# Second MLP product of round 4 moved to three one-pass products, each round's second product a round behind its first, and a new instruction order

## The chip, the cores and the metric

One core of a Trainium2 chip runs the whole kernel. The metric is device time in microseconds, the median of the timed runs. Engines: TensorE (PE: matmuls, and weight loads as PEld), VectorE (DVE), ScalarE (ACT), GpSimd (POOL) and SyncE (SP, which issues nearly all DMAs).

## What is computed

An RWKV-6 attention followed by a layer norm and an MLP with a residual, all in float32, on 4 sequences of 768 steps, 8 heads of 48, model width 384, hidden width 1536:

```
for t in range(S):                                   # per batch and head
    cur = outer(u * k[t], v[t])
    y[t] = r[t] @ (state + cur)
    state = w[t][:, None] * state + outer(k[t], v[t])
x  = y, heads joined to (4, 768, 384)
xn = (x - mean) / sqrt(var + 1e-6) * g_ln
out = x + relu(xn @ w_ch1) @ w_ch2
```

## The kernel before

**Rounds.** The 3072 steps are cut in 8 rounds of 384 steps (`RN`), each three tiles of 128 (`TT`). A round has an attention part (`front`: loads, inner products of four steps, transposes, four levels of `quads` and `grow`, `states`, `outputs`) and an MLP part (`back`: `normalize`, `turn_x`, then `mlp`). The first product has 12 blocks f of 128 hidden units (`FC`), each a PSUM bank `h_ps`; the second sums over the 12 blocks into three output tiles i.

**Two kinds of product.** A full float32 matmul, or three one-pass matmuls on values split beforehand into a high part H, a low part L and a combination D (names `xhl`, `xd`, `wh`, `wl`, `w1diff` for the first product, `hH`, `hL`, `hD`, `w2h`, `w2l`, `w2d` for the second). Rounds 1 to 7 take the first product in one-pass form (`THREE = 1`). Rounds from `LAST = NR - 3` = 5 on take the second in one-pass form too (`thirds`); rounds 0 to 4 use full matmuls `o<-ffn,h`. The third of the split weights `w1diff` goes to DRAM once and is streamed back for every block (`stream`).

**The one-pass second product before.** In `thirds`, ScalarE writes H from the bank `h_ps` (Relu), VectorE writes L from the same bank and then D. The three take the twelve homes "h". Each output tile has two sums: D's in one bank (the minus part) and L's and H's in another. Tiles 0 and 1 take the two-bank homes "a" (which attention uses until its end), tile 2 two homes "b", each a bank of its own. After the last block VectorE adds the two sums to x (`add`, `rest`) and SP stores the tile. In the last round's last block `go_d` and `go` are planned apart for all three tiles.

**What sets the order.** `Plan` collects operations with their needs and buffers; the list `ORDER`, written out in the file, says in which order they are issued, and for some which of two engines takes them (an entry over 10000 names the second engine). Buffers come from `HOMES`. Every engine works its own queue in this order. Where TensorE would pause for more than 0.35 us by the plan, matmuls on zeros named `idle` are put in. All engine instructions are recorded by one helper, so every row of the profile says L47; tiles tell them apart.

## Time and profile before

| | |
|---|---|
| median of 3 runs | 494.89 us (493.52 to 494.91) |
| the profiled execution | 493.06 us, span 491.2 us |
| busy PE / PEld | 480.1 us (98%) / 402.2 us (82%) |
| busy DVE / ACT / POOL | 352.8 us (72%) / 256.3 us (52%) / 105.5 us (21%) |
| TensorE clock granted | 1.00 over the span |
| DMA | 56.21 MB, mean 114 GB/s |
| full second products `o<-ffn,h` | 360 records, 125.2 us busy |

A page row gives engine, operation, output and inputs, count, then busy time and mean duration of one, then the idle time of the engine just before the group and what ended it. A full float32 matmul leaves two records. The `idle` matmuls count as busy.

### The profile page before, as it was taken

The numbers are of one execution on the slowest core, as the hardware profiler recorded it, in microseconds if no ns is written. First come the engines' busy times: TensorE is split into PE (matmuls) and PEld (weight loads), VectorE is DVE, ScalarE is ACT, GpSimd is POOL, SyncE is SP. The second block draws the span as 40 slices with busy tenths as digits, with TensorE's granted clock in tenths as the row PEclk, the third lists the DMA queues.
The fourth block names the chain that finished last, engine by engine and source line by source line (L and its number), as shares of the span: only waits on it lengthen the run. The fifth ranks groups of instructions, "written<-read, shape, count | busy, mean of one in ns | idle before, by whom it ended". The sixth has DMA issues, their size and how long they took to land.

```text
span 491.2 us, 17021 instructions
## 1 busy us (share of the span) xinstructions
PE 480.1 (98%) x7354; PEld 402.2 (82%) x7354; DVE 352.8 (72%) x735; ACT 256.3 (52%) x580; POOL 105.5 (21%) x107
## 2 busy tenths in 40 slices
PE   8998999999999999999999999999999999999995
PEld 4776887668987779966799667998679999999995
DVE  7998999999948999478737598366467766345334
ACT  2989988745573358434255712656454434332330
POOL 6423503612514026107700300000001100000000
PEclk9999999999999999999999999999999999999999
DMA  6777686377660455482177201740321142122201
GB/s 207 212 202 200 164 267 148 112 218 172 154 177 5 99 150 170 108 210 47 33 192 189 62 12 30 166 101 11 65 58 35 48 129 66 48 85 90 84 0 51
DMA packets 105435, 56.21 MB, mean 114 GB/s; under 512 B 61840, under 2 KB 102288, under 8 KB 105360
## 3 DMA queue, kind: packets, MB, share of 16 engines
q1 hardware_dynamic: 105088, 54.92, 42.4%
q8 instruction: 58, 0.95, 0.8%
q10 hardware_dynamic: 272, 0.20, 0.1%
q14 instruction: 17, 0.14, 0.1%
HBM read 45.27 MB, written 7.47 MB: 107 GB/s over the span
## 4 chain that ended last, share of the span: by engine, by line
PE 78%; DVE 7%; ACT 6%; DMA 3%; POOL 2%; issue 2%; SPq 1%; POOLq 0%; DVEq 0%; ACTq 0%
PE h_ps L47 28%; PE a L47 19%; PE o L47 19%; PE o_2P L47 3%; PE r_ps L47 2%; PE k_ps L47 2%; SPq L47 1%; PE xT_ps L47 1%; PE o_2D L47 1%; DMA raw<-in_moe_w_ch_dram 1%; PE kn_ps L47 1%; DVE A L47 1%; ACT k L47 1%; DVE vals L47 1%; ACT held L47 1%
## 5 line engine op out<-in xcount | busy, mean ns | idle before, releaser
L47 PE MATMUL o<-ffn,h 128*128 128x384 f32 x360 | 125.2, 489 | 0.1
L47 PEld LDWEIGHTS o<-ffn,h 128*128 128x128 f32 x360 | 65.0, 190 | 35.5 <-DVE ffn L47 0.4
L47 ACT ACTIVATE h_ps<-h_ps 128x384 f32<-128x384 f32 x84 | 39.4, 475 | 70.8 <-PE h_ps L47 67.8
L47 DVE SCALAR_TENSOR_TENSOR hL<-h_ps,hH 128x384 fp32r<-128x384 f32 x36 | 20.0, 557 | 50.3 <-ACT hH L47 50.2
L47 PE MATMUL h_ps<-xd,d 128*128 128x384 f32 x228 | 54.9, 353 | 0.4 <-DVE xd L47 0.3
L47 PE MATMUL h_ps<-xhl,wl 128*128 128x384 f32 x216 | 51.8, 348 | 0.0
L47 PE MATMUL h_ps<-xhl,wh 128*128 128x384 f32 x216 | 49.6, 337 | 0.0
L47 PEld LDWEIGHTS a<-r,k 48*56 48x56 f32 (+3 forms) x3072 | 39.4, 122 | 9.7 <-issue 5.9
L47 PE MATMUL a<-r,k 48*56 48x32 f32 (+3 forms) x3072 | 43.5, 208 | 0.5 <-DVE k L47 0.4
L47 ACT ACTIVATE h<-h_ps 128x384 f32<-128x384 f32 (+2 forms) x72 | 30.2, 441 | 23.6 <-PE h_ps L47 23.2
L47 PEld LDWEIGHTS h_ps<-xd,d 128*128 128x128 f32 x228 | 39.8, 188 | 2.9 <-issue 0.4
L47 PEld LDWEIGHTS h_ps<-xhl,wl 128*128 128x128 f32 x216 | 37.9, 188 | 1.1
L47 PEld LDWEIGHTS h_ps<-xhl,wh 128*128 128x128 f32 x216 | 38.8, 188 | 0.0
L47 DVE TENSOR_TENSOR r<-r,tot 112x768 f32<-112x768 f32 (+1 forms) x40 | 32.5, 817 | 7.2 <-PE a L47 7.2
L47 ACT ACTIVATE hH<-h_ps 128x384 fp32r<-128x384 f32 x36 | 17.7, 491 | 34.8 <-PE h_ps L47 34.8
L47 DVE TENSOR_TENSOR k<-k,tot 112x768 f32<-112x768 f32 (+1 forms) x40 | 32.4, 815 | 4.1 <-PE a L47 3.2
L47 PE MATMUL h_ps<-xf,w 128*128 128x128 f32 (+1 forms) x144 | 25.9, 333 | 0.1
L47 PE MATMUL a<-w2l,hL 128*128 128x384 f32 x72 | 24.4, 338 | 1.4 <-DVE x L47 1.4
L47 PE MATMUL idle<-nought 128*128 128x384 f32 (+2 forms) x74 | 24.8, 465 | 1.0 <-DVE eps L47 1.0
L47 ACT ACTIVATE xf<-xT_ps,g_sb 128x384 f32<-128x384 f32 (+2 forms) x27 | 14.5, 546 | 20.4 <-PE xT_ps L47 18.5
L47 DVE COPY_PREDICATED A<-mask,a 128x768 f32<-128x768 int8 (+2 forms) x27 | 24.1, 892 | 1.3 <-PE a L47 1.2
L47 ACT COPY k<-k_ps 112x512 f32<-112x512 f32 x24 | 14.1, 587 | 20.7 <-PE k_ps L47 20.6
(154 smaller groups left out, 1070.0 us busy)
## 6 DMA issues: line engine op xcount, KB each, us to landing
d<-w1d SPq DMA_DIRECT2D x84, 192.0 KB, 2.7
raw<-in_moe_w_ch_dram SPq DMA_DIRECT2D x24, 384.0 KB, 3.7
nat_w<-in_w_dram SPq DMA_DIRECT2D x24, 192.0 KB, 3.8
nat_r<-in_r_dram SPq DMA_DIRECT2D x24, 192.0 KB, 3.8
v<-in_v_dram SPq DMA_DIRECT2D x24, 192.0 KB, 3.5
nat_k<-in_k_dram SPq DMA_DIRECT2D x23, 192.0 KB, 3.7
out_dram<-x SPq DMA_DIRECT2D x5, 576.0 KB, 4.4
w1d<-w1diff SPq DMA_DIRECT2D x12, 192.0 KB, 2.8
```

Source lines behind the costliest of these rows:

```text
L47: ins = self.tc.keep_in_program_order(f(*args, **kw))
```

## The change

- `LAST` becomes `NR - 4`: round 4's second product is one-pass too (36 full products become 108 one-pass ones).
- The first product of a one-pass round now evicts h to SBUF (`relu`, homes "h", as in the other rounds). `thirds` makes H from that copy on ScalarE, L as a plain difference on VectorE or POOL, and D on VectorE; the three take the twelve homes "w2", in which the second product's weights stood before they were split.
- `back(rnd)` no longer calls `thirds`; it is planned after the next round's first products could begin, so that a round's second product lies about a round behind its first.
- The split weights of the second product get new places (`w2_place`), in buffers of the attention that are free by then.
- In the last block, only tile 2 has `go_d` apart from `go`.
- `idle`: the count at the start is worked out up to `WARMED` = 5.9 us.
- `ORDER` is a new list, for all engines. From how the instructions stand: on VectorE, round 1's inner products come earlier and the weights' joins later; the first normalised tile is the 86th VectorE instruction of the plan and was the 77th. The very first loads go r, r, w, ... where they went w, r, w, .... Of the 48 instructions that write L, 24 are on POOL.

```diff
-    THREE, LAST = 1, NR - 3
+    THREE, LAST = 1, NR - 4
...
+    def w2_place(n, f):
+        i = "HLD".index(n)
+        if f < 4 or 6 <= f < 10:
+            q = f >= 6
+            return ("k", "r", "A")[i], f"w2{n}{q:d}", 4, f - 6 * q
+        if f < 6:
+            return ("nk", "nr")[f - 4], f"xw2_{f}", 3, i
+        if f == 10:
+            return "v", "w2_10", 3, i
+        return ("tot", "w2_11", 2, i) if i < 2 else ("vx", "w2D_11", 1, 0)
...
         def high():
             ACT.activation(
-                out=tile_("h", H_, [P, RN], F32R), in_=tiles[h_], func=AF.Relu, scale=TOP
-            )
-        def low():
-            DVE.scalar_tensor_tensor(
-                out=tile_("h", L_, [P, RN], F32R), in0=tiles[h_], scalar=0.0,
-                in1=tiles[H_].bitcast(F32), op0=ALU.max, op1=ALU.subtract,
-            )
+                out=tile_("w2", H_, [P, RN], F32R), in_=tiles[h_], func=AF.Copy, scale=TOP
+            )
+        def low(e):
+            BY[e].tensor_tensor(
+                out=tile_("w2", L_, [P, RN], F32R), in0=tiles[h_], in1=tiles[H_].bitcast(F32),
+                op=ALU.subtract,
+            )
...
-        plan.add("ACT", 0.492, high, r=[h_], w=[H_], pri=at(rnd, 30))
-        plan.add("DVE", 0.557, low, r=[h_, H_], w=[L_], pri=at(rnd, 30), port=True)
+        plan.add("ACT", 0.522, high, r=[h_], w=[H_], new=[("w2", H_)], pri=at(rnd, 30))
+        plan.add(EITHER, (0.55, 1.0), low, r=[h_, H_], w=[L_], new=[("w2", L_)], pri=at(rnd, 30))
...
-            if last and rnd == NR - 1:
+            if last and rnd == NR - 1 and i == 2:
...
-            if rnd >= LAST:
-                thirds(rnd, f)
-                continue
             plan.add("ACT", 0.49, relu, r=[ps], w=[h_], pri=at(rnd, 30))
...
-        if rnd < LAST:
+        if rnd <= LAST:
             back(rnd)
     for f in range(FC):
         halve2(f)
     for rnd in range(LAST, NR):
-        back(rnd)
+        if rnd > LAST:
+            back(rnd)
+        for f in range(FC):
+            thirds(rnd, f)
```

## Prediction

> **What bounds the kernel now.** First the busy shares of the page, then three stages: the opening, the middle, and what is left once the last attention output of the last round is issued (TensorE, 368.23 us, two groups, done at 371.2).

> Stages (us, then busy time and instructions of each engine, granted clock, DMA share, GB/s):

> ```profile
> 0.00:48.80 48.80, 43.68 (x802) 31.58 (x802) 42.13 (x115) 36.45 (x88) 21.01 (x44) 1.00 0.75 204
> 48.80:371.20 322.40, 321.48 (x5906) 257.39 (x5899) 247.88 (x497) 179.18 (x406) 78.66 (x58) 1.00 0.47 119
> 371.20:491.20 120.00, 114.97 (x658) 113.23 (x654) 62.82 (x125) 40.71 (x87) 5.85 (x5) 1.00 0.21 65
> ```

> TensorE (first busy column) is full from 48.8 us on; VectorE (third) has 74 us to spare in the middle and 57 in the last stage. Who TensorE waits for:

> ```profile
> PE xT_ps L47 <- DVE xn L47: 2.3, 2, 2.2
> PE a L47 <- DVE x L47: 1.4, 1, 1.4
> PE idle L47 <- DVE eps L47: 1.0, 1, 1.0
> PE k_ps L47 <- POOL pad_k L47: 1.0, 1, 1.0
> ```

> Under 7 us in all. But a busy TensorE is not always one at work: it also runs "idle" matmuls. I therefore added up the useful matmuls in queue order at their rows' durations. Before 48.8 us they make 17.0 us, so 31.8 us are no work. That gap is 34.4 when the second output group of round 1 starts (62.1 us of work ahead of it, start 96.5), 36.7 at round 2's first group (114.5, 151.2), 40.3 at round 4's (209.0, 249.3), 45.3 at round 7's (322.9, 368.2). It grows by some 2 us a round, spread over the switches between small and full matmuls, with no stall. So in this kernel TensorE work taken away after 48.8 us comes off the end in full, if the opening keeps its pace and nothing new stalls.

> The rows that price the change:

> ```profile
> L47 PE MATMUL o<-ffn,h 128*128 128x384 f32 x360 | 125.2, 489 | 0.1
> L47 PE MATMUL a<-w2l,hL 128*128 128x384 f32 x72 | 24.4, 338 | 1.4 <-DVE x L47 1.4
> L47 ACT ACTIVATE h<-h_ps 128x384 f32<-128x384 f32 x48 | 22.7, 488 | 20.7 <-PE h_ps L47 20.4
> L47 POOL TENSOR_TENSOR w1diff<-wl,wh 128x384 fp32r<-128x384 f32 x7 | 8.4, 1206 | 11.0 <-DVE wl L47 11.0
> ```

> **1. The product of round 4.** In the chain three full products (six records) take 1.94 us, a few 2.13; three one-pass products take 0.53:

> ```profile
> 221.50 1.45 PE a L47 x96
> ...
> 225.98 3.89 PE o L47 x12
> ...
> 479.05 0.53 PE a L47 x3
> ```

> A round has 36 full products, 12 × 1.94 = 23.3 us; they become 36 × 0.527 = 19.0 (18.9 from six in 1.05). Gain 4.3; with one group in six at 2.13 it is 4.7. I take 4.4. [...]

> **2. The last tiles.** Before, the last product of tile 0 is split: the minus part first, then the rest, in the two banks of one tile. The chain shows what this did:

> ```profile
> 484.85 0.72 PE a L47 x4
> 485.57 0.34 issue
> 485.90 1.03 DVE x L47 x2
> 486.93 0.04 issue
> 486.98 0.63 PE a L47 x2
> 487.61 0.02 issue
> 487.63 0.56 DVE x L47
> ```

> The last two matmuls wait for VectorE's read of the other bank, and VectorE ends at 488.19. After, only tile 2, in banks of its own, is split; tiles 0 and 1 run whole. The same matmuls then end at 485.57 + 0.36 = 485.93, the two adds follow 0.33 later and take 1.03: 487.29. Gain 0.9. Bounds: 0 if VectorE still has tile 0's adds in hand (two at 0.55 ahead of tile 1's, but tile 0 ends two product groups earlier), 1.4 if all of the wait goes. Taken 0.9.

> **3. What rides along.** Rounds 5 to 7 evict h first (36 × 0.49 on ScalarE), and round 4 gains 12 high parts (0.52): 23.9 us more on ScalarE, whose busy time is 41 of the last 120 us. Round 4's 12 low parts, 12 differences and 3 more adds are 14.9 us on VectorE, with 57 spare there. The high part stands in ScalarE's queue ahead of the next shrink, for which TensorE's next first product waits; the cover is that thirds run behind their first product (the order has several other groups between). The bank of h_ps is read by one instruction instead of two; TensorE waits for no such bank now, so 0. The twelve "w2" homes hold H, L and D of four f, as "h" did. Round 4's one store of 576 KB becomes three of 192 KB; SP has only the streams of w1diff behind them, and DMA is at 0.21 there. All 0 in the sum; each costs what is shown below under the second rival if its cover is gone. In the new order round 7's attention is issued after 302 us of work instead of 323. [...]

> **4. The opening, found anew.** This is the unknown. Before, VectorE sets it: busy 42 of 48.8 us, and its waits are short ones:

> ```profile
> 13.36 1.03 DVE L47 TENSOR_TENSOR nat_k<-nat_k,nat_r 128x768 f32<-128x768 f32 x1 [1.35 <-ACT pad_k L47]
> 38.46 0.56 DVE L47 BATCH_NORM_STATS2 stats<-x 128x6 f32<-128x384 f32 x1 [1.85 <-ACT x L47]
> ```

> I added VectorE's instructions in queue order at row durations, less the 0.08 us by which neighbours overlap. Before, the first normalised tile is its 77th, 30.1 us of work, done at 40.76: a lag of 10.7. After, round 1's inner products stand ahead of it and the weights' joins behind: the first product of round 0 waits for the 94th, 41.1 us of work. The new place of the normalisation should avoid both waits above (3.2 us), and w's first load, now third in SP's queue (issued at about 2.3 instead of 0.8), costs about 0.6 of that again. So the lag is 8 to 10.7 and this product starts at 49.1 to 51.8, with 16.2 us of work ahead of it: a gap of 32.9 to 35.6, against 31.8. Check at round 1's second output group: VectorE's work up to its scan is the same (80.5 for 80.3), TensorE's work ahead of it is 57.3 for 62.1. With the old lag there (80.3 done at 94.85: 14.5) it starts at 96.7, a gap of 39.4 against 34.4: 5.0 lost. [...] Bounds 0.2 and 5.0. I take 1.5, nearer the low end, since both waits lie before the point.

> **Sum.** −4.4 − 0.9 + 1.5 = −3.8: span 487.4, and with the 1.86 us outside the span (493.06 − 491.2) 489.3. That execution stood 1.83 below the median of the timed runs, so the forecast is 494.89 − 3.8 = **491.1 us**, by itself 489.5 to 493.0.

> **Rivals.**
> *The opening eats the gain.* VectorE keeps its old lag, the new order has 4.8 us less TensorE work ready by round 1, and 5.0 go there: −4.4 − 0.9 + 5.0 = −0.3, 494.6. For it: VectorE's sums at that point are equal. [...]
> *POOL is late in the last rounds (slower).* Of the 48 low parts 24 now run on POOL, each between a high part and a difference that TensorE needs. The row above says 1.00 us undisturbed and up to 1.76 beside VectorE (w2d, alike, 1.2 on average). Toward the end a low part has some 0.7 us in hand: H9 of round 7 gets its home when f = 6 is done, and its product is about 3 us of TensorE work later, while high, low and difference take 0.52 + 1.0 + 0.55 and their hand-overs. If half of the 24 come 0.75 late: 9 us, 500.1; it decides from 3.8/24 = 0.16 us a piece on TensorE's path. Against: VectorE is half idle there and other groups stand between. [...]
> [...]

> **How the numbers follow.** 0.3% or 1.5 us is about what a measurement of this kernel tells from no change: faster is below 493.4, slower above 496.4. Chances: forecast 0.50, opening 0.20, POOL 0.15, more 0.15. Faster: 0.46 of the forecast's, all of the last, 0.03 of the opening's: 0.64. Same: the rest of the forecast's, 0.13 of the opening's, 0.02 of POOL's: 0.19. Slower 0.17. The range goes from 488.3 to 497.0, leaving out half of the last case and most of POOL's.

> **What would show it.** Right: TensorE's round-1 output groups near 91 to 94 us; o<-ffn,h falls from 360 records to 288 (72 per round); the last output group of round 7 near 350; no TensorE wait of over 1 us after it, and the two last adds back to back behind the last matmul. Wrong: round 1's groups at 96 or later; TensorE waiting for hL, hD or hH in the last 130 us; a VectorE or ScalarE wait between 250 and 350, where attention is now packed closer.

## The result, and the profile after

Four timed runs of each kernel, side by side: **490.02 us** (489.85 to 490.25) after, 494.2 (493.28 to 494.91) before, ratio 0.9917 (95% interval 0.9895 to 0.9939): 4.2 us less. The forecast was 491.1. The profiled execution, however, went only from 493.06 to 490.19 us, its span from 491.2 to 488.5: 2.75 us less by the unrounded spans (491.24, 488.48). Both are taken up below; they are not the same thing.

The stages of the changed kernel (us, then busy time and instructions of TensorE, its weight loads, VectorE, ScalarE and GpSimd, granted clock, DMA share, GB/s), the opening, the middle and the end. The last cut lies at the start of round 7's attention outputs here; before, it lay at their end (371.2):

```profile
0.00:48.80 48.80, 42.63 (x709) 30.66 (x713) 43.71 (x116) 34.96 (x79) 21.21 (x41) 1.00 0.72 192
48.80:350.00 301.20, 300.93 (x5775) 246.44 (x5766) 251.08 (x507) 178.09 (x410) 62.27 (x53) 1.00 0.52 130
350.00:488.50 138.50, 134.26 (x946) 133.29 (x945) 71.89 (x131) 60.98 (x138) 29.64 (x27) 1.00 0.18 57
```

TensorE is as full in the middle as before. From the start of round 7's outputs (350.13, before 368.38) to the end it is 138.35 us for 122.86, 15.5 more: round 4's second product and others now lie there. What TensorE waits for, longest first:

```profile
PE w_ps L47 <- POOL w L47: 1.2, 1, 1.2
PE w_ps L47 <- DVE w L47: 1.1, 1, 1.1
PE idle L47 <- DVE eps L47: 1.0, 1, 1.0
PE a L47 <- DVE k L47: 0.9, 1, 0.9
```

None is for `hH`, `hL` or `hD`, and the wait for `xn` (2.3) is gone. The product's rows, in the page's form (busy, mean ns of one, idle before):

```profile
L47 PE MATMUL o<-ffn,h 128*128 128x384 f32 x288 | 99.2, 488 | 0.0
L47 POOL TENSOR_TENSOR hL<-h,hH 128x384 fp32r<-128x384 f32 x24 | 26.8, 1127 | 86.8 <-PE o_2D L47 21.1
L47 DVE TENSOR_TENSOR hL<-h,hH 128x384 fp32r<-128x384 f32 x24 | 14.5, 606 | 13.7 <-PE o_2P L47 5.0
```

72 records (36 full products) have left `o<-ffn,h`. The end of the chain:

```profile
482.20 0.57 DVE x L47
482.77 0.02 issue
482.80 1.03 DVE x L47 x2
483.83 0.02 issue
483.85 1.03 DVE x L47 x2
484.88 0.02 issue
484.91 0.56 DVE x L47
```

No matmul waits for an add any more. All three tiles finish so close together that VectorE does the six adds in one row; it ends at 485.47, the last matmul at 484.27.

**Where the 2.75 us are.** I take the first `a<-last,r` matmul of the output groups of rounds 1, 3, 5 and 7, and subtract the useful TensorE work queued ahead of it at its rows' durations:

| | round 1 | round 3 | round 5 | round 7 |
|---|---|---|---|---|
| before: start, work | 91.91, 57.8 | 200.67, 161.7 | 303.44, 260.6 | 368.38, 322.9 |
| after: start, work | 93.68, 55.8 | 199.39, 157.0 | 293.87, 248.0 | 350.13, 302.2 |
| gap before | 34.1 | 39.0 | 42.8 | 45.5 |
| gap after | 37.9 | 42.4 | 45.9 | 47.9 |

The new opening is 3.8 us dearer at round 1 and 2.4 at round 7. The total of useful work falls from 440.4 to 436.1, by 4.3. From round 7's outputs to the end it is 122.86 us before and 138.35 after, 15.49 more for 16.4 more work: 0.9 less at the tail. −4.3 + 2.4 − 0.9 = −2.8.

This is one pair of profiles. A second profile of the changed kernel (fifth experiment) has a span of 489.8 us at the same clock, 1.3 more; between rounds 3 and 5, where two waits of 0.7 and 0.8 us marked "issue" lie, it loses 1.9. So the sum shows where the time lies, and 2.75 itself is good to about a microsecond.

### The profile page after: what moved, and what is told of

Its sections match the earlier page's. It is cut to its first block, busy times and chain, and to the rows that moved or that the text cites. A ratio compares the mean times of both kernels' runs of the same rounds, so it can differ in the third digit from the quotient of the medians.

```text
span 488.5 us, 17306 instructions
## 1 busy us (share of the span) xinstructions
PE 477.8 (98%) x7412; PEld 410.4 (84%) x7412; DVE 366.7 (75%) x753; ACT 274.0 (56%) x624; POOL 113.1 (23%) x120
## 4 chain that ended last, share of the span: by engine, by line
PE 87%; DVE 5%; SPq 1%; issue 1%; DMA 1%; DVEq 0%
PE h_ps L47 33%; PE a L47 23%; PE o L47 18%; PE o_2P L47 3%; PE r_ps L47 2%; PE o_2D L47 2%; PE xT_ps L47 2%; PE k_ps L47 2%; PE kn_ps L47 2%; SPq L47 1%; DVE A L47 1%; DVE s L47 1%; DVE x L47 1%; DVE k L47 1%; DMA d<-w1d 1%
## 5 line engine op out<-in xcount | busy, mean ns | idle before, releaser
L47 PE MATMUL o<-ffn,h 128*128 128x384 f32 x288 | 99.2, 488 | 0.0
L47 ACT ACTIVATE h<-h_ps 128x384 f32<-128x384 f32 (+2 forms) x108 | 47.7, 454 | 54.8 <-PE h_ps L47 54.2
L47 PEld LDWEIGHTS o<-ffn,h 128*128 128x128 f32 x288 | 52.3, 190 | 29.1
L47 ACT ACTIVATE h_ps<-h_ps 128x384 f32<-128x384 f32 x84 | 38.8, 475 | 49.0 <-PE h_ps L47 47.0
L47 DVE SCALAR_TENSOR_TENSOR hD<-hH,hL 128x384 fp32r<-128x384 f32 x48 | 30.4, 651 | 34.8 <-PE a L47 16.9
L47 PE MATMUL h_ps<-xd,d 128*128 128x384 f32 x204 | 50.0, 353 | 0.3 <-DMA d<-w1d 0.3
L47 PEld LDWEIGHTS a<-r,k 48*56 48x56 f32 (+3 forms) x3072 | 39.7, 122 | 10.1 <-issue 3.1
L47 POOL TENSOR_TENSOR hL<-h,hH 128x384 fp32r<-128x384 f32 x24 | 26.8, 1127 | 86.8 <-PE o_2D L47 21.1
L47 PE MATMUL a<-r,k 48*56 48x32 f32 (+3 forms) x3072 | 44.1, 208 | 1.1 <-DVE k L47 0.9
L47 PE MATMUL h_ps<-xhl,wl 128*128 128x384 f32 x180 | 43.8, 351 | 0.0
L47 DVE TENSOR_TENSOR k<-k,tot 112x768 f32<-112x768 f32 (+1 forms) x40 | 37.8, 947 | 5.9 <-PE a L47 4.5
L47 PE MATMUL h_ps<-xhl,wh 128*128 128x384 f32 x180 | 41.4, 338 | 0.0
L47 PEld LDWEIGHTS h_ps<-xd,d 128*128 128x128 f32 x204 | 35.4, 188 | 2.9 <-issue 0.9
L47 DVE TENSOR_TENSOR r<-r,tot 112x768 f32<-112x768 f32 (+1 forms) x40 | 34.1, 854 | 0.6 <-PE a L47 0.2
L47 PEld LDWEIGHTS h_ps<-xhl,wh 128*128 128x128 f32 x180 | 32.3, 188 | 0.0
L47 PEld LDWEIGHTS h_ps<-xhl,wl 128*128 128x128 f32 x180 | 31.0, 188 | 1.1 <-ACT h_ps L47 0.2
L47 PE MATMUL idle<-nought 128*128 128x384 f32 (+1 forms) x96 | 28.7, 425 | 1.0 <-DVE eps L47 1.0
L47 ACT ACTIVATE hH<-h 128x384 fp32r<-128x384 f32 x48 | 24.4, 522 | 8.0 <-PE a L47 3.5
L47 DVE COPY_PREDICATED A<-mask,a 128x768 f32<-128x768 int8 (+2 forms) x27 | 24.1, 893 | 5.6 <-PE a L47 5.5
L47 PE MATMUL h_ps<-xf,w 128*128 128x128 f32 (+1 forms) x144 | 26.0, 331 | 0.0
L47 PEld LDWEIGHTS idle<-nought 128*128 128x128 f32 x96 | 17.3, 200 | 9.1 <-issue 1.5
L47 DVE TENSOR_TENSOR hL<-h,hH 128x384 fp32r<-128x384 f32 x24 | 14.5, 606 | 13.7 <-PE o_2P L47 5.0
```

Source lines behind the costliest of these rows:

```text
L47: ins = self.tc.keep_in_program_order(f(*args, **kw))
```

## Experiments

Times are medians; where nothing else is said, before ran beside them, at 492.8 to 495.1. "The changed kernel" as a control (fifth experiment) gave 489.48.

**1. The old opening with the new rest.** The entries of `ORDER` up to round 1's second output group are the old ones:

```
-    ORDER = [3, 271, 2, 1, 12, 10, ...]            # new order
+    ORDER = [1, 3, 2, 10014, 13, ...,              # 580 entries of the old order
+             ...]                                  # the rest near the new order
```

> The changed kernel's code, but its order follows the old one instruction for instruction up to the last output group of round 1; the rest keeps roughly the new order, smoothed behind the seam. Theory (the opening cost more than the forecast's 1.5: net 2.65, and 4.1 where round 1 ends; TensorE work decides from there on): round 1's second output group is back at a gap of about 34.4 us between its start and the work queued ahead of it (new order: 38.5), and the gap saved stays to the end in good part: span 484.4 to 485.9, 2.6 to 4.1 less than the changed kernel, time about 486 to 487.5. Rival (what the old opening saves is lost again behind it, because TensorE then waits for VectorE, whose weight joins are still to be done): the gap is smaller at round 1 but equal by round 3; span 487.5 or more.

Measured: 495.04 (491.37 to 498.43), ratio 1.0031 (0.9998 to 1.0064); profiled span 490.4. At round 1 the lead is there: start 92.24, gap 34.4. At round 3 the gap is 42.5 (196.82, 154.3), the new order's. So the rival holds in its times: the lead is gone by round 3, 1.4 us of it right behind the seam. But the waits there are for ScalarE's `r` (two of 0.7, ended at 102.7 and 104.1) and not for VectorE, as the rival had it; where the rest goes is not shown. Eleven of the twelve runs had a clock of 0.985 to 0.995; the one at 1.0 took 492.49, so the clock alone does not explain it. That order is neither kernel's, so this run does not price the opening; it shows that the old opening can't be put ahead of the new rest for free.

**2. Round 4's product as one full matmul in place of three one-pass ones.**

```
             def both(i=i):
+                if rnd == LAST:
+                    PE.matmul(out_tiles(i)[0], tiles[H_].bitcast(F32)[:, ts(i, P)],
+                              w2_part("H", f).bitcast(F32), start=first, stop=last)
+                    return
```

> The changed kernel with round 4's three one-pass matmuls replaced in place by one full-precision matmul of the high parts (the low parts' products are left out, so the output is not the reference's); order, evictions and splits unchanged. Theory (TensorE work after 48.8 us goes to the end in full; a full product costs 0.647 against three of 0.176): 36 x (0.647 - 0.527) = 4.3 us slower than the changed kernel, 494.3. [...] Rival 'in the new order round 4 has slack on TensorE': under 2 us slower, below 492.

Measured: 493.84, against 489.43 for the third kernel on the same chip: 4.4 more. The chain of this kernel prices the product:

```profile
356.73 2.58 PE a L47 x8
```

Eight records are four full products: 0.645 each. From round 7's first `a<-last,r` (351.65) to the end it took 142.63 us, where the changed kernel takes 138.35: **4.28 more, and 36 × (0.645 − 0.527) = 4.25.** The theory holds, to the end in full. A full product costs 0.645/0.176 = 3.7 one-pass matmuls here.

**3. All low parts on VectorE.** The 24 entries of `ORDER` for `low` that name GpSimd lose their 10000.

> The changed kernel with all 48 low parts on VectorE: the 24 that ran on GpSimd (mean 1.13 us) are moved, nothing else. Theory (the low parts on GpSimd are off TensorE's path: no wait for hL, hD or hH in the trace): within 1 us of 490.0 either way; VectorE gains 24 x 0.55 = 13 us where it has over 60 idle. The forecast's rival (a low part that is late on GpSimd holds TensorE up): faster by 2 us or more, below 488.

Measured: 489.43, ratio 0.9919 (0.989 to 0.9948), where the changed kernel has 0.9917 and 0.9915. No change: the low parts on GpSimd were off TensorE's path. What they do cost shows in the rows of this kernel:

```profile
L47 DVE TENSOR_TENSOR hL<-h,hH 128x384 fp32r<-128x384 f32 x48 | 27.2, 580 | 24.1 <-PE a L47 10.2 <-ACT hH L47 6.1 <-PE o_2D L47 4.2
L47 DVE SCALAR_TENSOR_TENSOR hD<-hH,hL 128x384 fp32r<-128x384 f32 x48 | 26.7, 570 | 20.0 <-PE a L47 14.5 <-PE o_2P L47 3.6 <-PE o_2D L47 1.2
```

`hD` takes 570 ns a piece here and 651 in the changed kernel, 3.9 us of VectorE time over 48, all of it in cover. The means hide how: in the changed kernel six of the 48 take 1.18 to 1.37 us, here one does, and the others have about 0.55 in both. Each of these seven began while a GpSimd instruction ran and ended 0.41 to 0.42 us behind that instruction's end.

**4. The kernel before with tile 0 whole in the last block.**

```
-            if last and rnd == NR - 1:
+            if last and rnd == NR - 1 and i:
```

The entry of the separate piece falls out of `ORDER`, and the later numbers there move up.

> The kernel before with one edit: in the last round the last product of tile 0 is no longer split, so that VectorE's read of the minus bank stands behind all six matmuls; all else as before. Theory (the last two matmuls waited 1.43 us for a read of the other bank of their tile): the last two adds start together behind the last matmul, 0.9 us less than before (between 0.4 and 1.4), about 493.6 where before is 494.5. Rival (the adds of tile 2, still in VectorE's queue, set the end): no change, within 0.3 us.

Measured: 491.78, before 492.98, ratio 0.9971 (0.9949 to 0.9993). VectorE's last adds in this kernel:

```profile
483.43 0.55 DVE L47 SCALAR_TENSOR_TENSOR x<-o_2D,x 128x384 f32<-128x384 f32 x1
484.43 0.56 DVE L47 SCALAR_TENSOR_TENSOR x<-o_2P,x 128x384 f32<-128x384 f32 x1 [0.46 <-PE a L47]
484.91 1.14 DVE L47 SCALAR_TENSOR_TENSOR x<-a,x 128x384 f32<-128x384 f32 x2
```

The two last adds run together. From round 7's outputs to the end: 122.07, against 122.86 in the profile of before and 122.85 to 122.87 in two more profiles with that tail (sixth and ninth). That is 0.8, near the 0.9: tile 2's last add, still in the queue (the second line), may hold the other 0.1.

**5. The changed kernel again**, no edit.

> The changed kernel once more, as a control on the chip of these four runs, with more runs of both kernels. Expected: 489 to 490.5, ratio 0.992 +- 0.002, granted clock 0.998 to 1.0 in every run; the kernel before spreads over 491.8 to 496 with mean clocks from 0.987 to 1.0, its longer runs being those with the lower clock.

Measured: 489.48 (488.72 to 491.53), ratio 0.9915 (0.9888 to 0.9942); clock 0.998 to 1.0 in all six. Of before's 17 runs, 12 had a clock of 0.987 to 0.996, and all nine above 493.8 are among them. With the runs of before beside the first, eleventh and twelfth kernels there are 71: 37 with a mean clock of 0.997 or more, median **492.5**; 34 below it, median **494.7**. The changed kernel and those with its opening, or one near it (second, third, seventh, eighth), have 41 runs, every one at 0.997 or more.

**6. Before with the pause at 38.5 us filled.** The longest pause in the old opening is 2.16 us in before's profile, ahead of the first transpose of `xn`; nine more units of idle matmuls go there:

```
-    out.append(lambda n=n, home=home: idle[2](n, home[1]))
+    out.append(lambda n=n + 9 * (op.i == 97), home=home: idle[2](n, home[1]))
```

> The kernel before with one edit: nine more units of idle matmuls (about 1.9 us) where TensorE stands still for 2.4 us at 38.5 us, waiting for the first normalised tile. Theory (that pause makes the clock fall for a window of 3.4 us in some runs, and these are the kernel's longer ones): clock 0.997 or more in every run, the runs above 494 vanish, the median falls by 0.5 to 1.2 us against before, its fastest runs stay at 491.8. Rival (the spread comes from the loads, the clock only goes with it): spread and median as before, within 0.3.

Measured: 494.6, before 493.84; ratio 1.002 (0.9996 to 1.0044). The pause is filled (TensorE is busy for 3.40 of the 3.41 us from 38.85 on), yet six of twelve runs have 0.986 to 0.996 and 495.8 to 497.5. The theory falls: this pause alone is not what makes before's long runs long.

**7. w first.**

```
-    ORDER = [3, 271, 2, 1, 12, ...]
+    ORDER = [1, 3, 271, 2, 12, ...]
```

> The changed kernel with w's first load back at the head of SP's queue (order of the first loads as before). Theory (the opening is late because VectorE's first steps wait 1.5 us for w): the wait goes, the first product of round 0 starts 1 to 1.5 us earlier than 51.7, and the end with it: 0.8 to 1.5 us faster than the changed kernel in the same call. Rival (r and k then land later, and VectorE waits for these instead): no change within 0.4, the wait appears at another tile.

The changed kernel's wait that this aims at, from its timeline:

```profile
6.52 0.36 DVE L47 TENSOR_TENSOR pad_k<-nat_k,nat_w 128x192 f32<-128x192 f32 x1 [1.50 <-DMA nat_w<-in_w_dram]
```

Measured: 490.17 (488.36 to 490.89), the control 489.48 (488.72 to 491.53). In the profile the first product starts at 49.67 (50.2 to 51.7 in four profiles with w third) and round 1's outputs at 91.67 (92.2 to 93.7), so the opening does gain about 1.2. The time shows nothing of it: between rounds 3 and 5 alone, profiles of one and the same order differ by 2 us (94.0 to 96.4). Not settled.

**8. Another order for the changed kernel**, found by many small moves under the planner's own costs.

> The changed kernel with another order: the same operations, the listed order moved in many small steps so that by the planner's own costs each round's attention output comes about 1 us earlier from round 0 on. Theory (TensorE's queue alone decides once the opening is over, so an earlier opening passes to the end): round 1's first output group 0.7 us earlier than in the changed kernel (93.5), the end as much: 489.0 to 489.5. Rival (the planner's 1 us is below what its costs are wrong by): within 0.5 either way, with new waits for VectorE.

Measured: 490.1 (489.84 to 490.61): no gain. Round 1's first output group came at 94.97, not 0.7 earlier but 1.3 later than in the changed kernel. The rival holds: a planned microsecond is less than what the plan's costs are wrong by.

**9 and 10. Two more profiles, in search of the clock**: the kernel before, and the kernel of the first experiment, both without an edit.

> The kernel before, unchanged, for another profile: about half of its runs show a mean clock of 0.987 to 0.996 and are 1 to 4 us longer, and the profile on hand is one of the others. Theory (the new opening keeps the clock where the old one lets it fall): a run with the lower clock shows one to four windows of 3.4 us at half clock, all before 60 us, and the time lost there. Rival (the clock falls in the middle of the kernel): the windows lie behind 60 us, where the two kernels hardly differ.

> The first experiment's kernel (old order up to round 1's last output, then the new one), unchanged, for another profile: 11 of its 12 runs had a clock of 0.985 to 0.995. The same theory and rival as for the kernel before: windows at half clock before 60 us, and round 1's outputs later by what they cost (two windows or more, 97 us or later for the first), or windows behind 60 us.

Measured: 493.28 (clock 0.993) and 500.25 (0.986). Each row is a stretch of the trace; the third column from the right is the granted clock. Kernel before:

```profile
37.63:41.04 3.41, 1.05 (x8) 0.75 (x7) 2.54 (x6) 3.33 (x11) 0.67 (x2) 1.00 0.86 152
41.04:44.45 3.41, 3.41 (x75) 3.02 (x74) 2.89 (x10) 3.16 (x9) 0.86 (x1) 0.50 0.98 311
```

A stretch with 1.05 us of work is followed by one at half clock. Round 1 came 0.4 us later than in the first profile of before (92.31 for 91.91), the end 0.2 (span 491.45 for 491.24). The tenth:

```profile
102.60:106.00 3.40, 2.01 (x28) 1.23 (x26) 3.40 (x8) 2.07 (x4) 0.00 (x0) 1.00 0.84 232
106.00:109.40 3.40, 3.12 (x82) 2.75 (x83) 2.16 (x8) 0.53 (x2) 0.00 (x0) 0.50 0.81 161
...
341.50:344.90 3.40, 1.61 (x102) 1.49 (x95) 0.31 (x1) 2.62 (x7) 0.00 (x0) 1.00 0.12 40
344.90:348.30 3.40, 3.40 (x29) 3.31 (x21) 2.70 (x6) 1.16 (x3) 0.00 (x0) 0.50 0.43 86
```

Here the clock is at half from 41.1 to 44.6, from 106.0 to 112.8 and from 344.9 to 348.3. Time goes at the second and the third of these. Round 1 to round 3 takes 107.55 us, in the first experiment's profile, which kept the clock there, 104.58; round 5 to round 7 takes 61.76 for 58.13, with a wait of 1.79 us marked "issue" ahead of the window. The first experiment's profile has the same two waits for ScalarE; in stretches laid 3.41 us apart from its own at half clock (41.47 to 44.88), TensorE is busy for 2.74 and 2.41 us there, and the clock stays full:

```profile
99.49:102.91 3.42, 2.74 (x12) 1.65 (x13) 3.33 (x9) 2.15 (x5) 0.00 (x0) 1.00 0.51 133
102.91:106.32 3.41, 2.41 (x92) 1.88 (x93) 3.41 (x11) 2.01 (x4) 0.00 (x0) 1.00 0.74 195
```

So both readings hold in part: windows at half clock fall before 60 us and cost little, and behind it, at about 1.5 to 1.8 us each if all of these differences, less that wait, are theirs. The stretches at half clock in these two traces and in those of the first, eleventh and twelfth experiments are 3.4, 6.8, 13.7 and 17.1 us long, one, two, four and five times 3.41. Within one trace their starts lie whole numbers of 3.41 us apart, to 0.2 us (41.1, 106.0 and 344.9 in the tenth: 19 and 70 of them; 10.7, 34.6 and 266.7 in the eleventh: 7 and 68).

**11. The changed kernel without fillers between about 29 and 46 us.**

```
-                    out.append(lambda n=n, home=home: ...)
+                    if not 30 < t < 50:
+                        out.append(lambda n=n, home=home: ...)
```

> The changed kernel without the idle matmuls that fill TensorE's pauses between about 29 and 46 us; the rest of the order is untouched. Theory (in the new opening it is a TensorE that is hardly ever still that keeps the clock): the clock falls to half for one to four windows of 3.4 us right behind, mean 0.985 to 0.997, and the time grows by 1 to 5 us, 491 to 495. Rival (the fillers do nothing here): clock 0.998 or more, time within 0.5 us of 489.5, or a little less.

Measured: **506.25** (504.41 to 507.94), 16.8 above the control of the fifth experiment; mean clock 0.976 to 0.979. Far more than the theory's 5. The clock is at half from 10.7 to 14.1, from 34.6 to 48.2 and, right behind the longest of the waits below, from 266.7 to 270.1. But round 1's outputs start at 93.63, no later than in the changed kernel (93.68); the 14 us are lost behind it. TensorE's waits from 60 us on:

```profile
PE a L47 <- issue: 10.2, 9, 2.4
PE h_ps L47 <- ACT hH L47: 1.1, 1, 1.1
```

Nine waits, eight of them 0.65 to 2.4 us long, that no other engine ends, all in or beside stretches of small matmuls. The changed kernel has none above 0.5 there; the control has two, of 0.7 and 0.8.

**12. The same fillers, but narrow.** As many idle matmuls as in the changed kernel, those of that stretch 8 to 24 columns wide:

```
-                    out.append(lambda n=n, home=home: idle[2](n, home[1]))
+                    out.append(lambda n=n, home=home, t=t: idle[2](n, home[1], 8 if 30 < t < 50 else 128))
...
-    def idle(n, home):
+    def idle(n, home, cols=P):
...
-                t[:, 0 : now * P], zeros, nought.broadcast_to([P, now * P]), ...
+                t[:, 0 : now * cols], zeros, nought.broadcast_to([P, now * cols]), ...
```

> The changed kernel with the same idle matmuls as it has, in the same places and number, but those between about 29 and 46 us are 8 to 24 columns wide instead of 128 to 384: TensorE's queue holds the same instructions, and is still in the pauses. It parts two readings of the run without these matmuls, which took 506 us. Theory A (leaving them out moved where in TensorE's queue the pieces of its program end; the 10 us of waits marked 'issue' in the stretches of small matmuls, 95 to 365 us, come from that): those waits are as in the changed kernel, at most 2 us in all, and the time is 488.5 to 491.5, although the clock is at half for one to four windows between 34 and 48 us; round 1's first output group stays near 93. Theory B (a TensorE that is still in the opening costs the time, through its clock): 495 us or more, clock 0.976 to 0.985.

Measured: **491.55** (489.93 to 494.88), clock 0.977 to 0.986. TensorE's waits from 60 us on in this kernel:

```profile
PE h_ps L47 <- DMA d<-w1d: 0.3, 1, 0.3
PE a L47 <- DVE A L47: 0.3, 1, 0.3
PE a L47 <- issue: 0.2, 1, 0.2
```

The 10 us of "issue" are gone with the instructions back in their number, although the clock is at half for five windows, 33.3 to 50.3 us. Theory A holds in the main: it had said four windows at most, round 1's outputs near 93 (they came at 94.65) and 491.5 at most. 14.7 of the 16.8 us went with the instructions that were missing from TensorE's queue, and about 2 are left for the clock. (The two runs were on different chips; by their ratios to before, 1.025 and 0.9965, the first part is 14.)

What the waits are for, the traces tell, though "issue" names nothing. One DMA queue of the kind "instruction" (q8) brings 58 packets of 16 KB in every one of these profiles, one for each 254 to 256 of TensorE's recorded instructions. All 16 waits of TensorE marked "issue" that are 0.3 us or longer and lie behind 60 us, in six profiles (first, fifth, sixth, seventh, tenth, eleventh), end 1.2 to 1.6 us after one of these packets has landed; waits that another engine ended do so anywhere from 0.3 to 10 us after one. By these times TensorE waited for the next piece of its own program. Leaving 72 instructions out (36 matmuls and as many weight loads), at one packet for about 255, shifts where each later piece begins. That is not all that decides: the changed kernel's first profile has no such wait, its second has two.

## Why the prediction was right or wrong

- **What bounds the kernel** (TensorE's queue behind the opening): right. Work put back in the second experiment came through to the end to 0.03 us.
- **1, the product** (−4.4): right. 4.25 to 4.28 by the second experiment. Of the choice between 4.3 and 4.7, the lower end was the true one. The case "more" of the chances did not come: the price of a full product, 0.645, left no more than these 4.25 to come off.
- **2, the last tiles** (−0.9): right. 0.9 by the changed kernel's trace, 0.8 by the fourth experiment. The lower bound's reason, adds still in VectorE's hand, is there; the two figures leave 0.1 for it.
- **3, what rides along** (0): right. No wait for H, L or D in the trace, no change in the third experiment. The rival of GpSimd being late falls. The six `hD` of 1.18 to 1.37 us lie beside the path. "1.00 us undisturbed and up to 1.76 beside VectorE" was misread: all seven `w1diff` on GpSimd in the profile of before ran beside VectorE work, five at 1.00 us, one at 1.68 (84.47) and one at 1.76 (87.47). From 60 us on TensorE waits only once in the changed kernel's profile, for 0.3 us: VectorE and GpSimd do not hold it up there.
- **4, the opening** (+1.5): this term was mis-sized. It is 3.8 at round 1 and 2.4 at round 7; over the three profiles of the old opening unfilled and with its own rest (before, fourth, ninth) and four of the new one (after, second, third, fifth) the mean gaps at round 7 are 45.1 and 48.1, 3.0 apart. I had reckoned that both old waits (3.2 us) go and that w's later load costs 0.6; the waits went, but w cost 1.50 and 0.43, and the first product came at 51.7, the late end of my 49.1 to 51.8. No run shows the lower bound of 0.2, near which I took the term; the traces show 2.4 to 3.8 in its place. "The opening eats the gain" was thus more than half true. Of its signs, the first output group of round 1 came at 93.7, between 91 and 94; the second, at which I had priced the term, came at about 95, between what I had called right and wrong.
- **The sum** was −3.8 and is −2.75.
- **From the profile to the median: the step that failed unseen.** I took the 1.83 us by which before's profiled execution lay under its median as something that the change leaves alone. Most of it is probably clock, though the runs of that median have no clock on record. In later runs before's executions at a mean clock of 0.997 or more have a median of 492.5, the others 494.7; all 10 runs of the changed kernel are at 0.998 or more, median 489.86, and its profiled execution lies 0.17 above its first median. Clock is not all that parts a profiled execution from its median: in the second and fifth experiments it lies 2.2 and 2.0 us above, at a clock of 1.0. Like with like, the change is 492.53 − 489.86 = 2.67 us, the 2.75 of the profile; the rest of the 4.2 goes with the clock, which the new order lost in none of its runs. So one error took 1.05 us too much off, the other left 1.83 on, and 0.3 more lies in the 0.17 and in the time outside the spans (1.82 before, 1.71 after): 491.1 for 490.0 is a sum right in its large terms and lucky in the rest.
- **Still open:** what starts the windows in before's runs at 0.987. No profile of such a run was caught. The pause at 38.5 us alone isn't it (sixth); the first experiment's kernel, which has this opening and another rest, loses them behind round 1 (tenth). And whether the 1.2 us of w's place can be had.

No version here beats the changed kernel by more than the runs scatter.

## What to carry to other kernels

Where one engine's queue sets the time, a product's price can be taken from the rows to a few hundredths of a microsecond per piece, and comes through in full (here 4.28 us for the 4.25 of the rows); the order of the opening can't (here 2.4 to 3.8 for 1.5), so give it the whole range that its rows allow. Before you subtract a sum from a median, ask why the profiled run lies off the median: list every run's granted clock, because a new order may change that as well. And an edit that takes instructions out of TensorE's queue moves all behind it (here 36 idle matmuls fewer went with 16.8 us, and narrow ones in their place took 14.7 of these away): before you blame what was taken out, put back as many that do nothing.
